# Three fused blocks on one core: q and k fetched ahead of two moves, the last weight conversions split, token stores declared independent, and each expert's rows gathered a unit sooner

## The chip, the cores and the metric

The kernel runs on one core of a Trainium2 chip. A core has TensorE (PE in the rows; its weight loads are PEld), VectorE (DVE), ScalarE (ACT), GpSimd (POOL) and SyncE (SP), each with its own instruction queue, and 16 DMA engines that carry transfers between HBM and the on-chip memories. SP issues nearly all loads, POOL the transfers with indices and the stores of converted weights. The metric is device time in microseconds of one execution. Three runs of the kernel before gave 932.81 (median), 929.98 and 934.12.

## The reference

Attention with a causal mask and a bias from cumulative sums; its output, with heads side by side, is the token matrix of an expert layer (each token goes to the one expert with the largest logit), and that output goes through a dense feed-forward with a squared ReLU. The weights of the last block, `w_in` and `w_out`, arrive in float64; the rest is float32. q, k and v are (4, 8, 576, 64), s is (4, 8, 576), the tokens (2304, 512), the eight experts' `w1` (512, 1024) and `w2` (1024, 512) each, `w_in` (512, 2048), `w_out` (2048, 512).

```python
scores = scale * np.matmul(q, k.transpose(0, 1, 3, 2))
cum = np.cumsum(np.maximum(s, 0.0), axis=-1)
bias = -(cum[:, :, :, None] - cum[:, :, None, :])
scores = np.where(causal, -1e9, scores + np.minimum(bias, 0.0))
attn = softmax(scores);  out = np.matmul(attn, v)
e_idx = np.argmax(x @ w_gate, axis=1)
for e in range(E):
    ye = np.maximum(x[mask] @ w1[e], 0.0) @ w2[e]
    out[mask] = gate_w[mask, None] * eom[mask, e, None] * ye
r = np.maximum(x @ w_in, 0.0);  return (r * r) @ w_out
```

## The kernel before

Every float32 matmul operand is split into a high and a low part (`xt[:, 0]`, `xt[:, 1]`; `h`, `w` likewise), and three products are summed. The program has three stages, which follow each other.

**Attention (to about 250 us).** Work goes by 16 pairs of heads. For a pair, `load_qk` (lines 353 and 356) fetches q and k in four DMAs (for each, 128 x 2 x 256 and 64 x 2 x 64 floats), `order_qk` (line 373, on POOL in most pairs) lays them out as `qr` and `kr`, TensorE transposes them (lines 404, 408), and ScalarE and VectorE write the high and low parts into the two operand tiles `sta` and `stb`. The low and high rows are then spread within and between these tiles by DMAs on SP (`move`, line 441): three into `stb` from `sta` (`spread_b`), two within `sta` (`spread_a`). `load_aug` (lines 393, 394) adds the four rows of the bias to each tile. The score matmuls (line 490) read `sta` and `stb`; then come the maximum, the exponential, transposes of the probabilities (line 550) and the products with v (line 588). `load_v` is lines 380 and 383, the finished rows go to `x_d` in HBM at lines 726 and 730, and the first expert weights are brought in at line 253 (`stg`).

**Experts (255 to 505 us).** Eight experts, each with eight units of 128 hidden columns. `gather` (line 282, on POOL) brings the rows of an expert into `xr` by an index list, TensorE transposes them (line 1122), `emit_h` does the first product (line 1196), lines 1207 and 1208 take the ReLU and split `h`, `emit_y` does the second (line 1234). `put_tokens` (line 1390, on POOL) writes, by an index list, 20 blocks of the sorted list of tokens, `tok_d`, which the last stage needs. In the same stage VectorE, ScalarE and POOL turn the float64 weights into float32, in 32 pieces of 128 x 512: `cv_load` (SP), `cv_a` (line 1165 on VectorE, lines 1167 and 1168 on ScalarE: `cva`, `cvs`, `cvm`), `cv_b` (lines 1173, 1175 and 1177 on VectorE, then the products of lines 1178 and 1179 on POOL), `cv_store` (line 1184, a DMA on POOL into `w_in_d` or `w_out_d`). The expert weights come to `stg` (line 225) and are split into `w` (line 234 on ScalarE, line 238 on VectorE). The first 24 pieces are converted here, the last 8 in the next stage, where `cva`, `cvs` and `cvm` have one buffer each.

**Feed-forward (505 to 912 us).** Six tiles of 384 tokens, 16 units each: line 1196, then lines 1213 (ACT, `r`), 1214 (DVE, `r`), 1216 (ACT, `h`) and 1217 (DVE, `h`), then line 1241. Rows go to their tokens' places at line 1273, with a memset of a small tile `gap` between stores (line 1276).

**What sets the order.** Within a stage, each piece of work is put on a list with a number by `at(key, fn)`, and `emit_tasks` sorts the list and emits it; the instructions of each engine stand in that order. In the attention the numbers come from a table `K_` and the pair's base `t0`; a change of `ldqk` moves `load_qk` of every pair whose number is not bounded by the ordering of the pair two before. In the other stages a number is a count of units. A tile framework adds the semaphore waits: an instruction waits for those whose data or buffers it needs, and a DMA that writes a tensor waits for an earlier DMA that writes the same tensor.

Of the kernel before, what the change touches and what calls it, by code (L numbers as in the profile page):

```python
# [18 lines left out]
AF = mybir.ActivationFunctionType  # L19
# [26 lines left out]
    order=[0, 1, 3, 11, 2, 10, 4],  # L46
# [2 lines left out]
    LE=1.22,  # L49
    LV=0.63,  # L50
    vact=[[0], [1], [1], [1], [0], [1], [1, 1]],
    ldqk=-13.2,
    ldv=-3.41,
    scq=-4.19,
    sck=-5.35,
# [16 lines left out]
    cvb=0.4,  # L72
# [14 lines left out]
def attention_moe_ffn_kernel(  # L87
# [122 lines left out]
    def at(key, fn, *args):  # L210
        tasks.append((key, len(tasks), fn, args))
# [84 lines left out]
    with tc.manual_schedule():  # L296
# [862 lines left out]
        def cv_a(n):  # L1159
            t = cv[n][0]  # L1160
            a = cv_p.tile([P, 512], I32, tag="cva", name="cva")
            sq = cv_p.tile([P, 512], F32, tag="cvs", name="cvs", bufs=2 if n < NCV else 1)
            m = cv_p.tile([P, 512], F32, tag="cvm", name="cvm", bufs=2 if n < NCV else 1)
            mid = t.rearrange("p n z -> p (n z)").bitcast(U16).rearrange("p (n z) -> p n z", z=4)[:, :, 1]
            nc.vector.tensor_scalar(
                out=a, in0=t[:, :, 1], scalar1=3, scalar2=0x3FFFFFFF, op0=ALU.logical_shift_left, op1=ALU.bitwise_and)
            nc.scalar.activation(out=sq, in_=t.bitcast(F32)[:, :, 1], func=AF.Square)
            nc.scalar.activation(out=m, in_=mid, func=AF.Copy, scale=2.0 ** -36)
            cv[n] += [a, sq, m]

        def cv_b(n):
            t, a, sq, m = cv[n]
            nc.vector.scalar_tensor_tensor(
                out=a, in0=t[:, :, 1], scalar=-0x40000000, in1=a, op0=ALU.bitwise_and, op1=ALU.bitwise_or)
            nc.vector.scalar_tensor_tensor(
                out=sq, in0=sq, scalar=2.0 ** -30, in1=a.bitcast(F32), op0=ALU.is_ge, op1=ALU.mult)
            nc.vector.tensor_single_scalar(out=a, in_=sq.bitcast(I32), scalar=-0x800000, op=ALU.bitwise_and)  # L1177
            nc.gpsimd.tensor_tensor(out=m, in0=m, in1=a.bitcast(F32), op=ALU.mult)  # L1178
            nc.gpsimd.tensor_tensor(out=m, in0=sq, in1=m, op=ALU.add)  # L1179
            cv[n] = m  # L1180
# [196 lines left out]
        def pos_tokens():  # L1377
# [7 lines left out]
                out=pos_i.rearrange("p b t -> p (b t)"), in0=x, in1=rk_all.rearrange("p b t -> p (b t)"), op=ALU.add)  # L1385
            nc.vector.tensor_copy(out=tok[:, :, :, 1].bitcast(F32), in_=gsq)

        def put_tokens(b, t):
            n = P if t < NB - 1 else TAIL
            nc.gpsimd.indirect_dma_start(  # L1390
                out=tok_d[:, :], out_offset=bass.IndirectOffsetOnAxis(ap=pos_i[0:n, b, t:t + 1], axis=0),
                in_=tok[0:n, b, t, :], in_offset=None)

        def get_tokens():
            nc.sync.dma_start(out=tok_m, in_=tok_d.rearrange("(m p) z -> p m z", p=P))
# [32 lines left out]
        for g in range(E):  # L1428
# [4 lines left out]
                for c in range(len(rows_of(g + 1))):  # L1433
                    x_trans(g + 1, c, n0 + K_['xt0'] + K_['xt1'] * c, 0.3)
            if g + 2 < E:
                at(n0 + 6.5, gather, g + 2)
            hj = half_jobs(g + 1, "a") + half_jobs(g + 1, "b")
            at(n0 + 2.15, alloc_next)
            at(n0 + 2.15, alloc_next)
# [11 lines left out]
        if wide:  # L1451
            for n in range(NCV):
                t = K_['cvp'] * n + K_['cv0']
                at(max(t - K_['cvl'], 0.0), cv_load, n)
                at(t, cv_a, n)
                at(t + K_['cvb'], cv_b, n)
                at(t + K_['cvb'] + 0.01, cv_store, n)
        at(NS - 11.4, load_xf, 0)
        at(NS - 7.7, xf_hi, 0)
# [30 lines left out]
        if wide:  # L1490
            for i, n in enumerate(range(NCV, len(pieces))):
                t = 2.1 * i + 1.5
                at(t - 1.6, cv_load, n)
                at(t, cv_a, n)
                at(t + 0.2, cv_b, n)
                at(t + 0.21, cv_store, n)
        for i, job in enumerate(half_jobs(E + 1, "a") + half_jobs(E + 1, "b")):
            ta = 3.5 + 2.1 * i if i < 4 else 6.9 + 4.2 * (i - 4)
            w_job(job, ta - 1.2, ta, ta + 0.3)
# [107 lines left out]
```

## Time and profile before

| | |
|---|---|
| median of three runs | 932.81 us (929.98 to 934.12) |
| profiled execution | 931.6 us, of it the span 929.7 us |
| TensorE busy | 867.6 us (93%) |
| VectorE, ScalarE, POOL busy | 528.6, 446.3, 283.8 us |
| mean granted clock of TensorE | 0.975 |
| moved by DMA | 123.87 MB, mean 133 GB/s |

Times are counted from the start of the span. In the rows, `q<-in_q_dram` reads "into q from in_q_dram", xN is the number of instructions that a row sums up, and what stands in brackets is the idle time of the engine just before and who ended it. A row of the windows gives the stretch and its length, then for PE, PEld, DVE, ACT and POOL the busy time and the instructions, then the granted clock, the busy share of the 16 DMA engines, and GB/s. The granted clock is a share of TensorE's full clock; 0.50 is the lower of its two levels.

### The profile page before, as it was taken

How to read it: one execution, taken by the hardware profiler on the slowest of the kernel's cores; microseconds unless marked ns; L12 is line 12 of the kernel's file. 1: busy time of each engine (PE TensorE's matmuls, PEld its weight loads, DVE VectorE, ACT ScalarE, POOL GpSimd, SP SyncE). 2: the span in 40 equal slices, each digit the busy share in tenths (PEclk: the TensorE clock that was granted, in tenths of full speed). 3: DMA queues.
4: the chain of work that ended last, by engine and by line, in shares of the span. 5: the costliest groups of instructions: out<-in, count | busy, mean ns of one | idle time of the engine just before them, and what ended most of it. 6: DMA issues, size and time to landing. Idle time of an engine off the chain costs nothing.

```text
span 929.7 us, 15091 instructions
## 1 busy us (share of the span) xinstructions
PE 867.6 (93%) x5397; PEld 761.8 (82%) x5397; DVE 528.6 (57%) x1166; ACT 446.3 (48%) x985; POOL 283.8 (31%) x311
## 2 busy tenths in 40 slices
PE   7999998889989999998987899999999999999992
PEld 5777766667589989998987798999999999989991
DVE  8777666667758787887695666332323322322220
ACT  6677677778436556555654444232322323222220
POOL 5333143532236577767540244011001001001001
PEclk9999899999999999999998999999999999999996
DMA  5667677777158888888966642220000100000001
GB/s 151 160 155 177 164 172 193 188 191 187 37 181 277 253 251 282 279 232 271 305 221 195 199 151 71 68 68 15 25 29 35 35 1 35 1 1 35 1 1 37
DMA packets 87572, 123.87 MB, mean 133 GB/s; under 512 B 33601, under 2 KB 58177, under 8 KB 86594
## 3 DMA queue, kind: packets, MB, share of 16 engines
q1 hardware_dynamic: 80978, 103.77, 40.4%
q0 software_dynamic: 6224, 18.01, 5.4%
q10 hardware_dynamic: 288, 1.05, 0.4%
q8 instruction: 45, 0.74, 0.3%
q14 instruction: 37, 0.30, 0.1%
HBM read 83.12 MB, written 23.17 MB: 114 GB/s over the span
## 4 chain that ended last, share of the span: by engine, by line
PE 32%; issue 30%; DMA 16%; ACT 6%; DVE 5%; POOL 4%; SPq 3%; POOLq 0%; DVEq 0%; ACTq 0%
PE z L1196 10%; PE z L1241 6%; DMA stb<-sta 4%; PE z L1234 3%; PE s L490 3%; DMA cv<-in_moe_w_in_dram 3%; PE t L588 3%; PE t L550 2%; DVE w L238 2%; ACT p L534 2%; POOL out_dram L1273 2%; DMA sta<-aug_d 1%; DMA cv<-in_moe_w_out_dram 1%; DMA stg<-in_moe_w_dram 1%; SPq L441 1%
## 5 line engine op out<-in xcount | busy, mean ns | idle before, releaser
L1196 PE MATMUL z<-xt,w 128*128 128x384 f32 (+6 forms) x1920 | 338.5, 325 | 6.3 <-DVE r L1214 3.0
L1196 PEld LDWEIGHTS z<-xt,w 128*128 128x128 f32 x1920 | 316.0, 190 | 16.3 <-DVE h L1208 3.4
L1241 PE MATMUL z<-w,h 128*128 128x512 f32 x864 | 214.9, 393 | 0.0
L1241 PEld LDWEIGHTS z<-w,h 128*128 128x128 f32 x864 | 160.7, 188 | 29.3
L1214 DVE SCALAR_TENSOR_TENSOR r<-z,r 128x384 f32<-128x384 f32 x96 | 53.3, 555 | 168.2 <-ACT r L1213 168.2
L1213 ACT ACTIVATE r<-z 128x384 f32<-128x384 f32 x96 | 47.0, 490 | 168.2 <-PE z L1196 166.4
L1234 PE MATMUL z<-h,w 128*128 128x304 f32 (+5 forms) x768 | 117.6, 302 | 8.2 <-ACT h L1207 5.9
L1234 PEld LDWEIGHTS z<-h,w 128*128 128x128 f32 x768 | 109.6, 191 | 9.4 <-ACT h L1207 6.3
L238 DVE TENSOR_TENSOR w<-stg,w 128x1024 fp32r<-128x1024 f32 x72 | 109.8, 1525 | 8.5 <-ACT w L234 8.2
L1273 POOL DMA_INDIRECT out_dram<-ysb,tok_m x18 | 17.4, 964 | 314.7 <-ACT ysb L1260 312.4
L234 ACT CAST w<-stg 128x1024 fp32r<-128x1024 f32 x72 | 75.5, 1049 | 70.5 <-DMA stg<-in_moe_w_dram 50.0
L1217 DVE TENSOR_TENSOR h<-r,h 128x384 fp32r<-128x384 f32 x96 | 56.7, 590 | 55.6 <-ACT h L1216 55.6
L534 ACT ACTIVATE p<-p,nm 128x128 f32<-128x128 f32 (+3 forms) x144 | 84.3, 590 | 4.2 <-DVE nm L517 4.1
L517 DVE CUSTOM_DVE_ANT_0 p<-s,mask 128x128 f32<-128x128 f32 (+3 forms) x128 | 59.8, 486 | 45.9 <-PE s L490 45.0
L1216 ACT CAST h<-r 128x384 fp32r<-128x384 f32 x96 | 49.3, 513 | 73.4 <-DVE r L1214 73.4
L1178 POOL TENSOR_TENSOR cvm<-cvm,cva 128x512 f32<-128x512 f32 x32 | 44.1, 1377 | 100.3 <-DVE cva L1177 59.1
L550 PE MATMUL t<-ident,p 128*128 128x128 f32 x400 | 69.5, 289 | 2.1 <-ACT pt L569 0.7
L490 PE MATMUL s<-sta 68*128 68x192 f32 (+7 forms) x204 | 51.7, 350 | 14.9 <-DMA sta<-aug_d 13.2
L550 PEld LDWEIGHTS t<-ident,p 128*128 128x128 f32 x400 | 47.1, 145 | 15.3 <-ACT p L534 7.2
L1179 POOL TENSOR_TENSOR cvm<-cvs,cvm 128x512 f32<-128x512 f32 x32 | 58.9, 1841 | 2.5
L588 PE MATMUL t<-pt,v 128*64 128x320 f32 (+4 forms) x448 | 53.1, 368 | 0.0
L569 ACT COPY pt<-t 128x512 f32<-128x512 f32 (+1 forms) x94 | 46.8, 514 | 12.2 <-PE t L550 7.1
(218 smaller groups left out, 957.3 us busy)
## 6 DMA issues: line engine op xcount, KB each, us to landing
stg<-in_moe_w_dram SPq DMA_DIRECT2D x56, 512.0 KB
cv<-in_moe_w_out_dram SPq DMA_DIRECT2D x16, 512.0 KB
stb<-sta SPq DMA_DIRECT2D x14, 576.0 KB
cv<-in_moe_w_in_dram SPq DMA_DIRECT2D x14, 512.0 KB
xr<-yT_d SPq DMA_DIRECT2D x6, 768.0 KB
q<-in_q_dram SPq DMA_DIRECT2D x16, 256.0 KB
k<-in_k_dram SPq DMA_DIRECT2D x16, 256.0 KB
v<-in_v_dram SPq DMA_DIRECT2D x32, 128.0 KB
```

The source lines that it names most:

```text
L234: nc.scalar.copy(out=w_parts(job)[0], in_=raw[job])
L238: nc.vector.tensor_tensor(out=lo, in0=raw.pop(job), in1=hi.bitcast(F32), op=ALU.subtract)
L490: nc.tensor.matmul(ps[0:mw, d0:d0 + nn], lhsT=ql[r, m0:m0 + mw], rhs=kl[r, c0:c0 + nn], start=(i == 0 and (tail or n == 0)), stop=(done an ...
L517: nc.vector.tensor_tensor_reduce(out=dst, in0=src, in1=msk, scale=-1.0, scalar=3.0e38, op0=ALU.add, op1=ALU.min, accum_out=nm[:, c:c + 1])
L534: nc.scalar.activation(out=pt[:, cs], in_=pt[:, cs], func=AF.Exp, scale=-1.0, bias=nm[:, c:c + 1], accum_out=rs[:, r:r + 1])
L550: nc.tensor.transpose(tp[:, i * P:(i + 1) * P], pt[:, j0:j0 + P], ident)
L588: nc.tensor.matmul(o[64 * hd:64 * hd + 64, c0:n], lhsT=vt[r0:P, jb, hd, :], rhs=pt[r0:P, hd, jb, c0:n], start=(jb == 0), stop=(jb == last))
L1179: nc.gpsimd.tensor_tensor(out=m, in0=sq, in1=m, op=ALU.add)
L1196: nc.tensor.matmul(ps[:, 0:n], lhsT=wa[:, zw, kk, fl * P:(fl + 1) * P], rhs=xt[:, zx, kk, 0:n], start=(i == 0), stop=(i == 3 * KD - 1))
L1217: nc.vector.tensor_tensor(out=ht[:, 1, 0:n], in0=gg, in1=ht[:, 0, 0:n].bitcast(F32), op=ALU.subtract)
L1234: nc.tensor.matmul(y_acc[g][d][:, 0:n], lhsT=wb[:, zw, fl, d * P:(d + 1) * P], rhs=ht[:, zh, 0:n], start=(f == 0 and i == 0), stop=(f == n ...
L1241: nc.tensor.matmul(acc, lhsT=ht[:, zh, c * P:(c + 1) * P], rhs=wb[:, zw, fl, :], start=(f == 0 and i == 0), stop=(f == nf - 1 and i == 2))
```

## The change

There are four edits.

1. `ldqk` goes from -13.2 to -16.83, so `load_qk` is emitted earlier than `spread_a` of the pair before.
2. `cv_a` and `cv_b` of a conversion are split: `cv_m` is ScalarE's scaling (`cvm`), `cv_c` POOL's two products. In the expert stage all stand where they stood. For the last eight pieces, `cv_m` goes from t to t + 1.15, the rest from t + 0.2 to t + 1.3 units.
3. Each store of tokens is declared independent of the stores before it (the positions are distinct), and a memset of `gap` follows each on POOL.
4. The gather for expert g + 2 goes from 6.5 to 5.5 units into expert g.

```diff
--- before.py
+++ after.py
@@ -49,7 +49,7 @@
     LE=1.22,
     LV=0.63,
     vact=[[0], [1], [1], [1], [0], [1], [1, 1]],
-    ldqk=-13.2,
+    ldqk=-16.83,
     ldv=-3.41,
     scq=-4.19,
     sck=-5.35,
@@ -1165,8 +1165,10 @@
             nc.vector.tensor_scalar(
                 out=a, in0=t[:, :, 1], scalar1=3, scalar2=0x3FFFFFFF, op0=ALU.logical_shift_left, op1=ALU.bitwise_and)
             nc.scalar.activation(out=sq, in_=t.bitcast(F32)[:, :, 1], func=AF.Square)
-            nc.scalar.activation(out=m, in_=mid, func=AF.Copy, scale=2.0 ** -36)
-            cv[n] += [a, sq, m]
+            cv[n] += [a, sq, m, mid]
+
+        def cv_m(n):
+            nc.scalar.activation(out=cv[n][3], in_=cv[n].pop(), func=AF.Copy, scale=2.0 ** -36)
 
         def cv_b(n):
             t, a, sq, m = cv[n]
@@ -1175,6 +1177,10 @@
             nc.vector.scalar_tensor_tensor(
                 out=sq, in0=sq, scalar=2.0 ** -30, in1=a.bitcast(F32), op0=ALU.is_ge, op1=ALU.mult)
             nc.vector.tensor_single_scalar(out=a, in_=sq.bitcast(I32), scalar=-0x800000, op=ALU.bitwise_and)
+            cv[n] = a, sq, m
+
+        def cv_c(n):
+            a, sq, m = cv[n]
             nc.gpsimd.tensor_tensor(out=m, in0=m, in1=a.bitcast(F32), op=ALU.mult)
             nc.gpsimd.tensor_tensor(out=m, in0=sq, in1=m, op=ALU.add)
             cv[n] = m
@@ -1385,11 +1391,17 @@
                 out=pos_i.rearrange("p b t -> p (b t)"), in0=x, in1=rk_all.rearrange("p b t -> p (b t)"), op=ALU.add)
             nc.vector.tensor_copy(out=tok[:, :, :, 1].bitcast(F32), in_=gsq)
 
+        tputs = []
+
         def put_tokens(b, t):
             n = P if t < NB - 1 else TAIL
-            nc.gpsimd.indirect_dma_start(
+            put = nc.gpsimd.indirect_dma_start(
                 out=tok_d[:, :], out_offset=bass.IndirectOffsetOnAxis(ap=pos_i[0:n, b, t:t + 1], axis=0),
                 in_=tok[0:n, b, t, :], in_offset=None)
+            nc.gpsimd.memset(gap, 0.0)
+            for old in tputs:
+                tc.declare_no_dep(put.ins, old.ins, reason="each token has its own place in the sorted order")
+            tputs.append(put)
 
         def get_tokens():
             nc.sync.dma_start(out=tok_m, in_=tok_d.rearrange("(m p) z -> p m z", p=P))
@@ -1433,7 +1445,7 @@
                 for c in range(len(rows_of(g + 1))):
                     x_trans(g + 1, c, n0 + K_['xt0'] + K_['xt1'] * c, 0.3)
             if g + 2 < E:
-                at(n0 + 6.5, gather, g + 2)
+                at(n0 + 5.5, gather, g + 2)
             hj = half_jobs(g + 1, "a") + half_jobs(g + 1, "b")
             at(n0 + 2.15, alloc_next)
             at(n0 + 2.15, alloc_next)
@@ -1453,7 +1465,9 @@
                 t = K_['cvp'] * n + K_['cv0']
                 at(max(t - K_['cvl'], 0.0), cv_load, n)
                 at(t, cv_a, n)
+                at(t, cv_m, n)
                 at(t + K_['cvb'], cv_b, n)
+                at(t + K_['cvb'], cv_c, n)
                 at(t + K_['cvb'] + 0.01, cv_store, n)
         at(NS - 11.4, load_xf, 0)
         at(NS - 7.7, xf_hi, 0)
@@ -1492,8 +1506,10 @@
                 t = 2.1 * i + 1.5
                 at(t - 1.6, cv_load, n)
                 at(t, cv_a, n)
-                at(t + 0.2, cv_b, n)
-                at(t + 0.21, cv_store, n)
+                at(t + 1.15, cv_m, n)
+                at(t + 1.3, cv_b, n)
+                at(t + 1.3, cv_c, n)
+                at(t + 1.31, cv_store, n)
         for i, job in enumerate(half_jobs(E + 1, "a") + half_jobs(E + 1, "b")):
             ta = 3.5 + 2.1 * i if i < 4 else 6.9 + 4.2 * (i - 4)
             w_job(job, ta - 1.2, ta, ta + 0.3)
```

TensorE's order is the same in both kernels. The first place is SP's queue in one of the later attention pairs; `sta_134` and `stb_136` are the pair's operand tiles, `in_q_dram` and `in_k_dram` the inputs. Before:

```order
L441 DMA stb_136<-sta_134 64x2304
L441 DMA stb_136<-sta_134 64x576 x2
L253 DMA stg<-in_moe_w_dram 128x512
L441 DMA sta_134<-sta_134 64x576 x2
L393 DMA sta_134<-aug_d 4x576
L394 DMA sta_134<-aug_d 4x576
L353 DMA q<-in_q_dram 128x2x256
L356 DMA q<-in_q_dram 64x2x64
L353 DMA k<-in_k_dram 128x2x256
L356 DMA k<-in_k_dram 64x2x64
L253 DMA stg<-in_moe_w_dram 128x512
```

and now:

```order
L441 DMA stb_136<-sta_134 64x2304
L441 DMA stb_136<-sta_134 64x576 x2
L353 DMA q<-in_q_dram 128x2x256
L356 DMA q<-in_q_dram 64x2x64
L353 DMA k<-in_k_dram 128x2x256
L356 DMA k<-in_k_dram 64x2x64
L253 DMA stg<-in_moe_w_dram 128x512
L441 DMA sta_134<-sta_134 64x576 x2
L393 DMA sta_134<-aug_d 4x576
L394 DMA sta_134<-aug_d 4x576
L253 DMA stg<-in_moe_w_dram 128x512
```

The four fetches stand ahead of the weight load and the two moves within `sta`, right behind the moves into `stb`. The same holds for ten pairs; in six of them no load of `stg` stands there.

The second place is POOL's queue in the expert stage, around the gather for expert 6 (`tok_d` is the token list, `xr` the gathered rows, `cvm` a conversion's result). Before:

```order
L1184 DMA w_out_d<-cvm 128x512
L1390 DMA tok_d<-tok,pos_i 2304x2 x2
L1178 TENSOR_TENSOR cvm<-cvm,cva 128x512
L1179 TENSOR_TENSOR cvm<-cvs,cvm 128x512
L1184 DMA w_out_d<-cvm 128x512
L1390 DMA tok_d<-tok,pos_i 2304x2
L1178 TENSOR_TENSOR cvm<-cvm,cva 128x512
L1179 TENSOR_TENSOR cvm<-cvs,cvm 128x512
L1184 DMA w_out_d<-cvm 128x512
L282 DMA xr<-x_d,tbl_p 128x512 x2
L282 DMA xr<-x_d,tbl_p 16x512
```

and now:

```order
L1190 DMA w_out_d<-cvm 128x512
L1398 DMA tok_d<-tok,pos_i 2304x2
L1401 MEMSET gap 128x1
L1398 DMA tok_d<-tok,pos_i 2304x2
L1401 MEMSET gap 128x1
L1184 TENSOR_TENSOR cvm<-cvm,cva 128x512
L1185 TENSOR_TENSOR cvm<-cvs,cvm 128x512
L1190 DMA w_out_d<-cvm 128x512
L282 DMA xr<-x_d,tbl_p 128x512 x2
L282 DMA xr<-x_d,tbl_p 16x512
L1398 DMA tok_d<-tok,pos_i 2304x2
L1401 MEMSET gap 128x1
```

The three DMAs of the gather stand ahead of a token store and of a conversion's products and store, where they stood behind them. The gathers for experts 3 and 7 move past a token store and a conversion in the same way; those for experts 4 and 5 keep their place among the conversions.

The third place is ScalarE's queue in the feed-forward, around the second of the last eight conversions (numbers tell buffers apart; `cv` is the piece as loaded). Before:

```order
L234 CAST w2_6680<-stg_6864 128x1024
L1167 ACTIVATE cvs_6896<-cv_6862 128x512
L1168 ACTIVATE cvm_6897<-cv_6862 128x512
L1213 ACTIVATE r_6905<-z6_6872 128x384
L1216 CAST h_6904<-r_6905 128x384
L1213 ACTIVATE r_6943<-z7_6916 128x384
L1216 CAST h_6942<-r_6943 128x384
L234 CAST w3_6681<-stg_6901 128x1024
L234 CAST w2_6680<-stg_6940 128x1024
L1167 ACTIVATE cvs_6974<-cv_6938 128x512
L1168 ACTIVATE cvm_6975<-cv_6938 128x512
```

and now:

```order
L234 CAST w2_6700<-stg_6877 128x1024
L1167 ACTIVATE cvs_6916<-cv_6875 128x512
L1219 ACTIVATE r_6924<-z6_6892 128x384
L1222 CAST h_6923<-r_6924 128x384
L1171 ACTIVATE cvm_6917<-cv_6875 128x512
L1219 ACTIVATE r_6957<-z7_6929 128x384
L1222 CAST h_6956<-r_6957 128x384
L234 CAST w3_6701<-stg_6920 128x1024
L234 CAST w2_6700<-stg_6953 128x1024
L1167 ACTIVATE cvs_6994<-cv_6951 128x512
L1219 ACTIVATE r_6999<-z6_6963 128x384
```

The scaling into `cvm` stands behind the next tile's `r` and `h`, where it stood right behind the square into `cvs`.

## Rows read from the trace of the kernel before

**Rows 1.** Waits on TensorE: waited for, total us, times, longest.
```profile
PE s L490 <- DMA sta<-aug_d: 13.2, 7, 2.8
...
PE z L1122 <- DMA xr<-x_d,tbl_p: 5.4, 3, 4.1
PE z L1196 <- DVE r L1214: 3.0, 1, 3.0
```

**Rows 2.** SyncE's timeline, three stretches: start, us, line, DMA, pieces.
```profile
59.02 3.61 SPq L441 DMA_DIRECT2D stb<-sta  x3
...
116.73 3.62 SPq L441 DMA_DIRECT2D stb<-sta  x3
122.66 1.11 SPq L441 DMA_DIRECT2D sta<-sta  x2
...
124.72 0.40 SPq L353 DMA_DIRECT2D q<-in_q_dram  x1
...
127.21 0.59 SPq L253 DMA_DIRECT2D stg<-in_moe_w_dram  x1
...
136.37 0.83 SPq L253 DMA_DIRECT2D stg<-in_moe_w_dram  x1
138.35 1.10 SPq L441 DMA_DIRECT2D sta<-sta  x2
...
194.69 3.54 SPq L441 DMA_DIRECT2D stb<-sta  x3
```

**Rows 3.** Windows: busy us (count) by engine, granted clock, DMA share, GB/s.
```profile
59.00:194.70 135.70, 121.90 (x914) 90.90 (x912) 89.15 (x323) 96.38 (x280) 46.41 (x57) 0.95 0.75 178
194.70:218.70 24.00, 23.95 (x192) 17.56 (x191) 18.15 (x62) 19.85 (x56) 9.01 (x8) 1.00 0.81 194
122.50:123.50 1.00, 1.00 (x11) 0.83 (x9) 0.93 (x8) 0.74 (x3) 0.12 (x1) 1.00 0.03 8
126.50:127.00 0.50, 0.50 (x4) 0.42 (x5) 0.00 (x0) 0.00 (x0) 0.00 (x0) 1.00 0.85 275
...
422.50:425.90 3.40, 3.22 (x14) 3.23 (x15) 1.03 (x3) 2.03 (x4) 1.89 (x2) 0.51 1.05 340
```

**Rows 4.** POOL's timeline, 313 to 334 us; idle before in brackets.
```profile
321.55 0.98 POOL L1390 DMA_INDIRECT tok_d<-tok,pos_i  x1 [6.01 <-DVE h L1208]
...
326.68 1.03 POOL L282 DMA_INDIRECT xr<-x_d,tbl_p  x1 [0.31 <-issue]
...
331.12 1.66 POOL L1390 DMA_INDIRECT tok_d<-tok,pos_i  x1 [0.31 <-issue]
```

**Rows 5.** The list of waits on POOL: the token stores.
```profile
POOL tok_d L1390 <- DMA tok_d<-tok,pos_i: 15.6, 6, 4.6
```

**Rows 6.** Groups by line on POOL: busy us, mean ns, idle before.
```profile
L1179 POOL TENSOR_TENSOR cvm<-cvs,cvm 128x512 f32<-128x512 f32 x32 | 58.9, 1841 | 2.5
L1178 POOL TENSOR_TENSOR cvm<-cvm,cva 128x512 f32<-128x512 f32 x32 | 44.1, 1377 | 100.3 <-DVE cva L1177 59.1 <-ACT h L1207 11.5 <-issue 11.0
...
L1276 POOL MEMSET gap<- 128x1 f32 x18 | 2.1, 115 | 0.0
```

**Rows 7.** The chain of waits, two stretches: start, us, what.
```profile
314.03 6.77 DMA tok_d<-tok,pos_i
...
415.18 7.45 DMA xr<-x_d,tbl_p
```

**Rows 8.** Timelines of VectorE and TensorE, 334 to 339 us.
```profile
334.13 0.43 DVE L1165 TENSOR_SCALAR cva<-cv 128x512 int32<-128x512 int32 x1 [2.23 <-POOL cvm L1178]
...
338.56 1.93 PE L1196 MATMUL z<-xt,w 128*128 128x304 f32 x12 [2.11 <-DVE h L1208]
```

**Rows 9.** Timelines of ScalarE and TensorE, 523 to 529 us.
```profile
523.35 0.66 ACT L1168 ACTIVATE cvm<-cv 128x512 f32<-128x512 uint16 x1 [2.80 <-DMA w_out_d<-cvm]
523.91 0.48 ACT L1213 ACTIVATE r<-z 128x384 f32<-128x384 f32 x1
...
525.03 3.86 PE L1196 MATMUL z<-xt,w 128*128 128x384 f32 x12 [3.00 <-DVE r L1214]
```

## The prediction

> **What bounds the kernel now.** I read the list of waits on TensorE first, because TensorE is the engine that sets the end, and asked of every long wait where it lies and who is late. The largest is 13.2 us in seven waits of the attention's score matmuls (line 490) for the loads of `sta`; the expert stage has 5.4 us in three waits of the row transposes (line 1122) for gathered rows; the start of the second feed-forward has one wait of 3.0 us for VectorE's `r` [rows 1]. The edits touch these three places and no other long wait, so I take them one by one.
>
> *Attention.* SyncE's timeline shows who paces a head pair. Behind the three moves that spread `stb` (issue ends at 116.73 + 3.62 = 120.35) SP stands still until they have landed and issues `sta` at 122.66: 2.31 us in which the queue does nothing. Only after `sta` come the four fetches of q and k, from 124.72 to 127.21, 2.49 us of issuing [rows 2]. In four late pairs a load of `stg` already stands in the wait (136.37, ends 137.20, `sta` at 138.35), which leaves 1.15 us of it [rows 2]. From the `stb` moves at 59.02 to those at 194.69 there are nine pairs in 135.67 us, 15.1 us each [rows 2]; the last two pairs, which have no q and k left to fetch, take 24.00 us, 12.0 each [rows 3]. TensorE is busy 121.9 of the nine pairs' 135.7 us at a granted clock of 0.95 and 23.95 of the last 24.00 us at 1.00 [rows 3]. So with the fetch in the queue SP sets the pair and TensorE waits; without it TensorE is the bound.
>
> *Experts.* POOL is one queue for token stores (line 1390), gathers (line 282) and the two conversion products (lines 1178, 1179). A store waits for the store ahead of it to land: issued at 314.03, landed 6.77 us later [rows 7], the next starts at 321.55 [rows 4]. The page names another releaser there, which had long been done, so I go by the landing. Six such waits come to 15.6 us [rows 5]. Two of them reach TensorE: a VectorE conversion waits 2.23 us for POOL at 334.13 and TensorE 2.11 us at 338.56 behind it [rows 8]; and the gather for expert 6 goes out only at 415.18, lands 7.45 us later [rows 7], and is the 4.1 us of [rows 1]. After that wait TensorE is granted 0.51 for 3.4 us [rows 3], the lower level (1.2 GHz).
>
> *Start of the second feed-forward.* `cvm` has one buffer; ScalarE's write of it at 523.35 waits 2.80 us for the store of the piece before, and the `r` that TensorE needs stands right behind it at 523.91; TensorE starts at 525.03 after 3.00 us, and slowly (3.86 us for 12 matmuls) [rows 9]. From 545 us on the feed-forward waits for nothing that an edit moves.
>
> **A: q and k fetched in front of `sta`.** Nothing is added or taken away: ten times four DMAs on SP, 2.49 us of issue, go into the wait for `stb`. In six pairs the free 2.31 us take nearly all of it, `sta` slips by about 0.2, and SP's loop is 2.2 us shorter; in the four late pairs 1.15 us are free, the loop is 1.2 shorter and `sta` is issued about 1.3 later. If SP alone set the pair: 6 × 2.2 + 4 × 1.2 = 18.0 us. The other end is lower than this. The q and k data now lie ahead of `sta` on the way to SBUF: two pieces of 128 x 2 x 256 and two of 64 x 2 x 64 floats are 0.59 MB, 2.1 us at the 275 GB/s at which they land now and 3.3 us at the stretch's mean of 178; the DMA engines are nearly idle in the wait (share 0.03 at 122.5 to 123.5), so about 1 us of that is free [rows 3]. So `sta` lands about 1 us later in an early pair and nearly 2 in a late one, a delay that eats the lead of the pairs but is paid again in each pair only where `sta`'s landing is itself the loop (the first rival). What TensorE can give back is the 13.2 us of waits and some of the lower clock behind them. I take 1.5 of 2.2 us in the early pairs and 0.6 of 1.2 in the late ones, where the DMA share is already 0.75 [rows 3]: 6 × 1.5 + 4 × 0.6 = 11.4, less part of the one slip: **−11 us**, range −5 to −15.
>
> **B: token stores that don't wait, gathers a unit sooner.** The 20 stores lose the wait for the one before; a memset of 0.115 us follows each, 2.3 us in all on POOL [rows 6], which idles elsewhere. The second store goes at about 315.6 instead of 321.55. But the gather of expert 3 (from 326.68 to 331.12, 4.4 us [rows 4]) now stands ahead of the store and the products that were at 321.55, so these start only 1 to 1.5 us sooner; the next products come some 5 us sooner, and the 2.23 us of VectorE and the 2.11 us of TensorE go: −2.1. The gather of expert 6 stands one store and one pair of products (1.4 + 1.8 us [rows 6], and a store) sooner, and the waits of the stores ahead of it are gone: out of 415.18 by at least 6 us, so that its 7.45 us of landing end before TensorE asks. That takes the 4.1 us, and half of the 3.4 us at half clock: −1.7. Together **−8 us**. Bounds: −4, where the gather's landing lengthens since more transfers run together (the landing of one gather is all I see), and −10, where the other waits for gathers (5.4 − 4.1 = 1.3 us) and a little clock come too.
>
> The landing is the row on which this rests: 6.77 us [rows 7]. The Trainium skill (DMA: Bandwidth & Descriptors, section Anatomy of one DMA — SWDGE (gpsimd) path) puts the fixed cost of a GpSimd DMA at about 2.0 us whatever its size; by that a store of a kilobyte would be down before the next starts, declaring the stores independent would be worth nothing, and the sum would be 2.1 us higher. This trace has three times that, so the row decides.
>
> **C: the last eight conversions later and in pieces.** ScalarE's scaling of the middle bits (`cvm`) moves from right behind the square to behind the next tile's `r` and `h`, and the bit work and products with it. The 3.0 us at 525.03 go with the clock drop behind them (1.7, by the 3.4 us at half clock of [rows 3]): −4.7. What is new: `cvs` and `cva` have one buffer as well, and the products of a piece, now later, must be done on POOL (3.2 us by the means [rows 6]) before ScalarE may square the next piece; the next `r` is queued behind that square, and TensorE waits for `r`. The store that is late at the start (it lands at about 523.3) pushes one piece into the next, so I expect two waits of nearly the POOL pair, 2.9 us each, until the pieces have caught up: +5.8. Bounds: −4.7 (no new wait) and +7 (two whole pairs, 6.4 us, and a clock drop behind each, 3.4, less 4.7 is 5.1; one store that lands late again adds about 2). Together **+1 us**, between ends far apart, since the wait that goes and those that come are of one kind and size.
>
> **Sum.** The profiled execution took 931.6 us (span 929.7 and 1.9 around it). 931.6 − 11 − 8 + 1 = 913.6; that execution lies 1.2 us under the median of 932.8, so 914.8, rounded to **915 us**. I add the terms whole, for the three stages follow each other and none overlaps another.
>
> **Rivals.** (1) *Slower: the fetch lengthens the pair.* `sta` can be issued only when `stb` is down and must land before the score matmuls; with 0.59 MB ahead of it this path grows by 2.1 − 1.0 = 1.1 us in ten pairs and by another 0.95 us in the four where 0.26 MB of `stg` is ahead too (at 275 GB/s): 11 + 3.8 = +14.8 in place of −11. With B and C: 932.8 + 14.8 − 7 = 941 us. It decides where the landing of `sta`, not SP's queue, closes the loop of a pair. For it speaks that TensorE's waits end on `sta` [rows 1]; against it that the last two pairs have the same moves and take 12 us [rows 3], and that the engines idle in the wait. The Trainium skill (DMA: Bandwidth & Descriptors, section Queues, rings and completion order) says that on each DMA engine the descriptors of one issuer are consumed in ring order, which is the premise of this rival: `sta` can't overtake the fetch. The share of 0.03 in [rows 3] shows the ring empty at that time, so the trace bears out only part of it. (2) *Attention gains nothing*: ScalarE's and VectorE's chains or the transfers take the place of SP. ScalarE is busy 96.4 of 135.7 us, the DMA engines 0.75 of it [rows 3], so there is room, but little in the late pairs. 932.8 − 7 = 926 us. (3) *The last conversions wait more often*: C is +5: 919 us. (4) *The stores wait all the same* (a bound on DMAs in flight, or the next gather behind them): then only the gathers' −5.8 are left of B: 917 us.
>
> **Chances.** Forecast 0.52, (1) 0.09, (2) 0.18, (3) 0.13, (4) 0.08. The forecast's own range is 906 to 922, from half of A's and C's bounds. For 8 in 10 the range reaches down to 903 (A −15, B −10, C −4.7 make 902 to 903) and up to 930, past (2) with a little of its spread; most of (1) stays out. A measurement of this kernel tells about 0.5% (4.7 us) from no change. Faster by more: nearly all of the forecast, (3) and (4) and four fifths of (2): 0.82. Within: the rest of (2) and a weak form of (1): 0.10. Slower: 0.08.
>
> **What would show it.** A: SP's timeline has q and k between `stb` and `sta`, the pairs are about 13.5 us apart, and the waits of line 490 for `sta` fall well below 13 us; if they grow, rival (1) is right. B: stores on POOL follow each other without a wait of 4 to 6 us, the gather of expert 6 goes out before 410 us on this trace's clock, and no granted clock of 0.5 stands near 422. C: no wait of TensorE for `r` at the first conversion but two shorter ones within the next 25 us. The forecast is wrong if the attention ends less than 5 us sooner, or if the feed-forward takes over 6 us more from its first matmul to its last.

## The result and the profile after

The changed kernel takes 919.9 us (median of four runs, 918.3 to 920.7) against 933.5 of the kernel before in the same comparison: a ratio of 0.986 with a 95% interval of 0.983 to 0.990, so 13.6 us or 1.4% faster. The forecast was 915, from 903 to 930. The profiled execution took 918.3 us, its span is 916.4.

TensorE's instructions stand in the same order in both kernels, so each matmul of one trace can be set beside the same matmul of the other. The difference of their starts, by place:

| the same matmul, before | after | ahead by | what lies between |
|---|---|---|---|
| 205.4 us | 192.9 | 12.5 | attention |
| 313.0 | 300.6 | 12.4 | experts 0 and 1 |
| 343.3 | 329.0 | 14.3 | the wait of [rows 8] |
| 424.3 | 404.2 | 20.1 | the gather for expert 6 |
| 464.7 | 451.5 | 13.2 | experts 6 and 7 |
| 513.3 | 497.8 | 15.5 | end of the experts |
| 529.9 | 509.7 | 20.2 | the first of the last conversions |
| 599.9 | 586.6 | 13.3 | the other conversions; constant from here on |

The gains came where the sum had put them, and two of them were partly given back within 50 us. Waits on TensorE, columns as in [rows 1]:

```profile
PE z L1240 <- ACT h L1213: 8.6, 3, 5.2
PE s L490 <- DMA sta<-aug_d: 5.9, 5, 2.8
PE z L1202 <- DVE r L1220: 4.0, 3, 2.3
...
PE z L1122 <- DMA xr<-x_d,tbl_p: 1.2, 1, 1.2
```

The waits for `sta` fell from 13.2 to 5.9 us and those for gathered rows from 5.4 to 1.2. The waits for `r` (3.0 before) grew, and so did those for ScalarE's `h`, which [rows 1] doesn't carry. Before they were:

```profile
PE z L1234 <- ACT h L1207: 5.9, 2, 5.1
```

The longest of them, 5.1 us at 495 us, is there in both kernels. (Lines behind the edits moved: 1196, 1207, 1208, 1214, 1234 and 1390 are now 1202, 1213, 1214, 1220, 1240 and 1398.)

**Attention.** SyncE's timeline of a pair, where [rows 2] had a standstill:

```profile
109.29 3.63 SPq L441 DMA_DIRECT2D stb<-sta  x3
113.02 0.74 SPq L353 DMA_DIRECT2D q<-in_q_dram  x1
...
115.24 0.65 SPq L356 DMA_DIRECT2D k<-in_k_dram  x1
116.33 1.15 SPq L441 DMA_DIRECT2D sta<-sta  x2
...
122.67 3.63 SPq L441 DMA_DIRECT2D stb<-sta  x3
```

From 112.92 to 116.33 SP issues the four fetches; only 0.44 us are left of the wait. The pair is 13.4 us long. The nine pairs that took 135.7 us in [rows 3] take 124.2 now, with TensorE at the full clock:

```profile
56.40:80.00 23.60, 23.48 (x182) 16.85 (x180) 15.81 (x55) 18.64 (x56) 7.85 (x8) 1.00 0.77 182
56.40:180.60 124.20, 116.96 (x925) 87.06 (x923) 91.01 (x326) 96.50 (x283) 48.40 (x58) 1.00 0.82 194
180.60:206.10 25.50, 25.39 (x200) 18.43 (x199) 19.41 (x66) 21.41 (x63) 9.00 (x8) 1.00 0.80 186
```

Of the 11.5 us, 6.6 are idle time that went (13.8 to 7.2 us beside the busy time), and 4.9 are busy time: 117.0 us instead of 121.9, for rather more matmuls (925 against 914), at a granted clock of 1.00 instead of 0.95. By `sta` and `stb` moves, five early pairs take 66.3 us (56.42 to 122.67) instead of 73.7 (59.02 to 132.75), 1.5 less each, and the four late ones 57.9 instead of 61.9, 1.0 less each.

**Experts.** On POOL the stores follow each other, and the gather for expert 6 goes out at 391.44:

```profile
380.57 1.01 POOL L1398 DMA_INDIRECT tok_d<-tok,pos_i  x1 [0.30 <-issue]
381.58 0.26 POOL L1401 MEMSET gap<- 128x1 f32 x1
381.88 0.97 POOL L1398 DMA_INDIRECT tok_d<-tok,pos_i  x1
...
391.44 1.11 POOL L282 DMA_INDIRECT xr<-x_d,tbl_p  x1 [0.30 <-issue]
```

That is 23.7 us sooner than the 415.18 of [rows 7], 11 more than the attention gave. TensorE takes these rows at 403.37 without a wait, and then stops for something else:

```profile
403.37 0.60 PE L1122 MATMUL z<-ident,xr 128*128 128x128 f32 x4
...
431.32 2.23 PE L1240 MATMUL z<-h,w 128*128 128x288 f32 x12 [2.91 <-ACT h L1213]
...
442.74 1.77 PE L1202 MATMUL z<-xt,w 128*128 128x272 f32 x12 [0.91 <-DVE h L1214]
```

The chain of waits of the changed kernel says what `h` was late for (start, us, what):

```profile
407.49 9.05 DMA stg<-in_moe_w_dram
...
418.32 1.23 DVE w L238
...
419.65 0.38 SPq L225
...
420.08 9.60 DMA cv<-in_moe_w_in_dram
...
430.34 0.64 ACT cvm L1171
430.98 0.30 ACT h L1213
```

A load of weights takes 9.05 us to land. SP's next load of weights (line 225) goes out only behind VectorE's conversion of it, the load of a conversion piece is queued on SP behind that, and it takes 9.60 us. ScalarE squares that piece and scales it ahead of `h`, and TensorE waits 2.91 us. The DMA engines are full in this stretch, and behind the wait the clock is granted at half (windows, columns as in [rows 3]):

```profile
433.10:436.50 3.40, 3.40 (x17) 3.40 (x16) 3.33 (x5) 3.15 (x7) 1.60 (x2) 0.50 0.53 166
410.00:420.00 10.00, 9.47 (x72) 9.06 (x71) 6.67 (x11) 4.52 (x10) 7.09 (x7) 1.00 1.00 271
420.00:430.00 10.00, 7.92 (x59) 7.42 (x57) 6.69 (x9) 3.06 (x6) 5.54 (x6) 1.00 0.90 252
```

**Last conversions.** ScalarE's timeline, which answers to [rows 9]:

```profile
506.95 0.68 ACT L1171 ACTIVATE cvm<-cv 128x512 f32<-128x512 uint16 x1 [0.68 <-DMA w_out_d<-cvm]
...
514.67 0.68 ACT L1167 ACTIVATE cvs<-cv 128x512 f32<-128x512 f32 x1 [4.57 <-POOL cvm L1185]
515.25 0.47 ACT L1219 ACTIVATE r<-z 128x384 f32<-128x384 f32 x1
```

The wait of 2.80 us for the store is 0.68 us now, but the next square waits 4.57 us for POOL's products, with `r` right behind it. TensorE waits for that `r`, and once more at 527.30:

```profile
516.37 2.37 PE L1202 MATMUL z<-xt,w 128*128 128x384 f32 x12 [1.44 <-DVE r L1220]
...
527.30 3.07 PE L1202 MATMUL z<-xt,w 128*128 128x384 f32 x12 [2.29 <-DVE r L1220]
```

### The profile page after: what moved, and what is told of

It is laid out like the page before. It is cut to its first block, busy times and chain, and to the rows that moved or that the text cites. A ratio compares the mean times of both kernels' runs of the same rounds, so it can differ in the third digit from the quotient of the medians.

```text
span 916.4 us, 15088 instructions
## 1 busy us (share of the span) xinstructions
PE 862.0 (94%) x5397; PEld 755.3 (82%) x5397; DVE 533.0 (58%) x1166; ACT 444.2 (48%) x985; POOL 284.0 (31%) x331
## 3 DMA queue, kind: packets, MB, share of 16 engines
q10 hardware_dynamic: 288, 1.05, 0.3%
## 4 chain that ended last, share of the span: by engine, by line
issue 33%; PE 26%; DMA 11%; DVE 10%; POOL 8%; ACT 5%; SPq 3%; POOLq 0%; DVEq 0%; ACTq 0%
PE z L1202 7%; DVE w L238 4%; PE z L1247 4%; PE z L1240 3%; DMA stg<-in_moe_w_dram 3%; PE s L490 3%; PE t L588 3%; PE t L550 2%; DMA sta<-aug_d 2%; POOL out_dram L1279 2%; POOL cvm L1185 1%; POOL cvm L1184 1%; DVE cva L1175 1%; SPq L441 1%; DVE cvs L1177 1%
## 5 line engine op out<-in xcount | busy, mean ns | idle before, releaser
L238 DVE TENSOR_TENSOR w<-stg,w 128x1024 fp32r<-128x1024 f32 x72 | 113.7, 1579 | 14.4 <-ACT w L234 14.4
L1240 PEld LDWEIGHTS z<-h,w 128*128 128x128 f32 x768 | 109.7, 191 | 11.5 <-ACT h L1213 9.3
L1223 DVE TENSOR_TENSOR h<-r,h 128x384 fp32r<-128x384 f32 x96 | 54.7, 569 | 55.6 <-ACT h L1222 52.7
L1184 POOL TENSOR_TENSOR cvm<-cvm,cva 128x512 f32<-128x512 f32 x32 | 42.1, 1316 | 123.4 <-DVE cva L1179 78.7
L550 PE MATMUL t<-ident,p 128*128 128x128 f32 x400 | 67.4, 281 | 2.2 <-ACT pt L569 0.7
L1185 POOL TENSOR_TENSOR cvm<-cvs,cvm 128x512 f32<-128x512 f32 x32 | 61.3, 1917 | 2.5
L550 PEld LDWEIGHTS t<-ident,p 128*128 128x128 f32 x400 | 45.2, 141 | 15.8 <-ACT p L534 7.9
```

What stands on the lines that cost most here:

```text
L238: nc.vector.tensor_tensor(out=lo, in0=raw.pop(job), in1=hi.bitcast(F32), op=ALU.subtract)
L550: nc.tensor.transpose(tp[:, i * P:(i + 1) * P], pt[:, j0:j0 + P], ident)
L1223: nc.vector.tensor_tensor(out=ht[:, 1, 0:n], in0=gg, in1=ht[:, 0, 0:n].bitcast(F32), op=ALU.subtract)
L1240: nc.tensor.matmul(y_acc[g][d][:, 0:n], lhsT=wb[:, zw, fl, d * P:(d + 1) * P], rhs=ht[:, zh, 0:n], start=(f == 0 and i == 0), stop=(f == n ...
```

## The experiments

Each ratio is to the kernel before in the same comparison; 0.1% is 0.93 us. Where a part stands alone, the rest is as before (in the runs of the four edits' parts the conversion helper is split but emitted where it was).

**q and k alone.**

```diff
-    ldqk=-13.2,
+    ldqk=-16.83,
```

> Of the four edits only the first (q and k fetched in front of the moves within sta); the conversion helper is split as in the changed kernel but emitted where it was. Theory (SP's queue sets the pair, and the fetch now hides in its wait): the attention ends 12 to 13 us sooner as in the changed kernel, the expert stage and the feed-forward are as long as before, so 12 to 13 us under the kernel before, about 921 us where the kernel before has 933.5. Rival (the expert stage is paced by transfers that run on their own clock, so that an earlier start is partly lost there): only 8 to 10 us. If the gain of the whole change came from the other edits: under 5 us.

Measured: 920.8 us, ratio 0.986 (0.982 to 0.991), some 13 us faster. That is the theory's figure, but the interval, 9 to 17 us, holds the upper half of the rival's 8 to 10 too. In the trace the attention is 11.6 us ahead at 205 us; the waits for gathers and `h`, still there, take part of it in the experts (5.3 ahead at 408, 7.5 at their end), and 9.2 are left at the end of the kernel, as the rival has it. So the attention's gain is shown, and whether the experts let all of it through is not.

**v in the wait instead of q and k.**

```diff
-    ldv=-3.41,
+    ldv=-2.85,
```

> The kernel before with one number changed: the three v fetches of a pair (0.29 MB, 2.6 us of issuing on SP) move from ahead of the stb moves into the wait between the stb and the sta moves, so v is fetched a little later than before; q and k stay where they were, behind sta. Theory (what counts is SP's issue time that leaves its loop, whatever is fetched): about 10 to 13 us under the kernel before, and SP's waits for stb at line 441 fall from 20.9 us to a few. Rival (what counts is that q and k arrive earlier): no gain, within 2 us of the kernel before. Second rival (0.29 MB ahead of sta delays its landing and that closes the loop): slower than before.

Measured: 921.5 us, ratio 0.987 (0.983 to 0.991), as much as with q and k, though v is fetched later and q and k stay where they were. SP's timeline:

```profile
109.10 3.67 SPq L441 DMA_DIRECT2D stb<-sta  x3
112.81 1.71 SPq L380 DMA_DIRECT2D v<-in_v_dram  x2
114.56 0.65 SPq L383 DMA_DIRECT2D v<-in_v_dram  x1
115.32 1.18 SPq L441 DMA_DIRECT2D sta<-sta  x2
```

The wait for `stb` no longer stands among SP's waits of the attention, and the nine pairs take 124.1 us, as with q and k alone (124.0), against 135.7 before. So it is SP's issue time that counts, not which data come sooner. This is the run that tells the two apart. (The profiled execution took 929.6 us, 8 over the median: it is 11.2 us ahead at 205 us, the experts take most of it back, and 2.2 are left.)

**Both in the wait.** Both numbers changed.

> The kernel before with both numbers of the attention changed: v, q and k of a pair (0.88 MB, some 5 us of issuing) all stand between the moves into stb and those within sta, where SP's queue waits only 2.3 us. Theory (SP's issue time sets the pair, and in the changed kernel SP no longer waits for stb, so nothing is left to hide): as q and k alone, 12 to 14 us under the kernel before. Rival (the fetch ahead of sta lengthens the path of a pair, and with q and k alone it was just short of deciding): sta is issued about 2.6 us later and lands 2 to 3 us later, the waits of TensorE for sta at line 490 grow to over 13 us, and the kernel is at least 8 us slower than with q and k alone.

Measured: 927.6 us, ratio 0.994 (0.990 to 0.997): faster than before, and 7 us (0.74%) slower than with q and k alone; the waits for `sta` are 10.0 us, against 5.8 with q and k alone. The early pairs are as short as with q and k alone (13.5 us here). The four late pairs, with the load of `stg` in the queue too, take 63.1 us (122.34 to 185.47), against 57.6 with q and k alone (122.38 to 180.01) and 61.9 before. My theory's "nothing is left to hide, so nothing changes" is wrong there. A late pair with q and k alone, on SP and TensorE:

```profile
137.27 3.58 SPq L441 DMA_DIRECT2D stb<-sta  x3
...
144.63 1.14 SPq L441 DMA_DIRECT2D sta<-sta  x2
...
149.98 0.45 PE L490 MATMUL s<-sta 68*128 68x192 f32 x2 [1.45 <-DMA sta<-aug_d]
```

and here:

```profile
138.15 3.63 SPq L441 DMA_DIRECT2D stb<-sta  x3
...
148.32 1.15 SPq L441 DMA_DIRECT2D sta<-sta  x2
...
153.95 0.45 PE L490 MATMUL s<-sta 68*128 68x192 f32 x2 [1.41 <-DMA sta<-aug_d]
```

From the moves into `stb` to those within `sta` it is 10.2 us instead of 7.4, and from there to the matmul that waits for `sta` 5.6 instead of 5.4. In the four late pairs `sta` goes out 2.3 to 3.7 us later, and where TensorE waits for it in both runs its landing takes 0.1 to 0.9 us more. So it is SP's issue time again, some 5 us in a wait of 2, that makes `sta` late, as the rival has it, and only to a small part the bytes ahead of it. The waits stayed under the rival's 13 us; its "at least 8 us" can't be told from the 7. What the bytes do shows with q and k alone: in the late pairs `sta` lands 5.4 to 5.5 us behind its issue, where it took 3.7 to 3.9 before with no fetch ahead. The Trainium skill (DMA: Bandwidth & Descriptors, section Queues, rings and completion order) has descriptors of one issuer consumed in ring order on each DMA engine. The late pairs are in line with that. The same section lets a later one finish its write before an earlier one, so the "can't overtake" of rival (1) is more than it states.

**Stores and gathers alone.** The third and fourth edit of the diff.

> Of the four edits only the third and fourth (token stores independent, gathers a unit sooner). Theory (the gathers' wait goes, and later waits for loads of weights and of conversion pieces, which share the DMA engines, take most of it back): the row transposes' waits of 5.4 us go to about 1, TensorE is 7 to 8 us ahead just behind the gather of expert 6, and 2 to 4 us are left at the end of the expert stage: 930 us where the kernel before has 933.5. Rival (the giving back in the changed kernel comes from its attention being shorter, not from these edits): 7 to 8 us are left, 926 us.

Measured: 928.6 us, ratio 0.995 (0.993 to 0.998), about 4.4 us faster by the ratio: the theory's 3.5 lies inside the interval, the rival's 7.5 does not. The trace shows the giving back without the shorter attention: 1.2 us ahead at 408 (in the kernel before's time), 6.9 at 424, 2.3 at 465, 4.7 at the end.

**Stores alone.** The third edit.

> Of the four edits only the third (token stores declared independent, with a memset behind each; gathers where they were). Theory (most of the gathers' lateness comes from stores that wait in front of them on POOL): 4 to 6 us under the kernel before, nearly as much as stores and gathers together (5.7), TensorE's wait for the gather of expert 6 gone or under 1.5 us. Rival (the place of the gathers does it): within 1.5 us of the kernel before, the wait of 4 us for the gather stays.

Measured: 925.3 us, ratio 0.992 (0.989 to 0.995), 5 to 10 us: the stores are most of the two, as the theory has it, and the gain is rather more than it asked for. The profiled execution took 931.8 us (the runs go from 921.4 to 931.8) and shows no gain at the end, so where the gain lies can't be read from it; in it the wait for gathered rows is 2.6 us at most instead of 4.1, so it shrank and did not go.

**Gathers alone.** The fourth edit.

> Of the four edits only the fourth (gathers from 6.5 to 5.5 units). Theory (the stores are most of it, as stores alone gave 6.8 us): 0 to 3 us under the kernel before; the gather of expert 6 stands past one store and one conversion, so its wait of 4.1 us on TensorE falls to under 1, and part of it is caught by later waits. Rival (either of the two is enough, the gain is the same wait): 5 to 7 us.

Measured: 930.4 us, ratio 0.998 (0.994 to 1.001): inside the 0 to 3 us of the theory, not clear of zero. In the trace the waits for gathered rows are not among the long ones, and TensorE gets 4.4 us ahead at the gather of expert 6 (between 408 and 424), all of them given back by 464 us. Stores alone are no worse than stores and gathers together; the overlap of the intervals leaves open whether the fourth edit adds anything.

**Last conversions alone.** The second edit.

> Of the four edits only the second (the last eight conversions later and in pieces). Theory (one wait of 3 us goes with its low clock, new waits for cvs buffers and the products come, more in sum): 1 to 3 us slower than the kernel before, with two or three waits of TensorE for r of 1 to 2.5 us each in the first 30 us of the feed-forward. Rival (the edit is a gain and the feed-forward's loss in the changed kernel comes from the stores still in flight behind a shorter expert stage): 1 to 4 us faster.

Measured: 934.5 us, ratio 1.002 (0.999 to 1.005): from 1.4 us faster to 4.4 slower. In the trace the wait of 3 us and its low clock go (4.8 us gained by the same matmuls from 513 to 530), two waits for `r` come, 3.2 us in sum, and 5.7 us are lost from there to 600: 0.9 us in sum, as C has it (−4.7 and +5.8).

**All but the conversions.** The second edit undone in the changed kernel.

> The changed kernel with the second edit undone (the last eight conversions back at their places; first, third and fourth edits stay). If the times add up as the parts did alone (about 13 us for the q and k fetches, 5 to 6 for stores and gathers): 18 to 19 us under the kernel before, about 915 us, 4 to 5 under the changed kernel. Theory that the expert stage gives back in company (behind the gathers TensorE runs into loads that are no sooner): 15 to 16 us under the kernel before, about 918 us, with a single wait for r at the start of the feed-forward as in the kernel before.

Measured: 915.4 us, ratio 0.982 (0.979 to 0.985), 16.9 us faster than before. With the changed kernel's 0.986 (0.983 to 0.990) the second edit cost about 4 us; the intervals just overlap. Parts apart (0.9861 and 0.9953) make 0.9815, so they may well add up; but the interval, 14 to 19.5 us, holds the 18 to 19 of adding up and the 15 to 16 of my theory alike.

**Bit work early.** In the changed kernel, for the last eight pieces:

```diff
-                at(t + 1.3, cv_b, n)
-                at(t + 1.3, cv_c, n)
-                at(t + 1.31, cv_store, n)
+                at(t + 0.2, cv_b, n)
+                at(t + 1.16, cv_c, n)
+                at(t + 1.17, cv_store, n)
```

> The changed kernel with VectorE's bit work (cv_b) of the last eight conversions back at t + 0.2, while the scaling stays at t + 1.15 and the products and the store come right behind it (t + 1.16, t + 1.17). Theory (the new waits come from products that are late for the single buffer of cvs, because the bit work stands late on VectorE): ScalarE's waits for POOL in front of the square (4.6 and 2.0 us in the changed kernel) go to about 1, TensorE's waits for r fall from 4.0 us to under 1.5, and the kernel is 3 to 5 us faster than the changed one, 915 to 917 us. Rival (the store that lands late sets it, whatever the products do): as the changed kernel, within 1 us.

Measured: 916.4 us, ratio 0.982 (0.978 to 0.985). The same rows of ScalarE, and POOL's first product (lines 1183, 1184 and 1218 are 1184, 1185 and 1219 of the changed kernel):

```profile
510.12 0.67 ACT L1171 ACTIVATE cvm<-cv 128x512 f32<-128x512 uint16 x1
510.88 1.28 POOL L1183 TENSOR_TENSOR cvm<-cvm,cva 128x512 f32<-128x512 f32 x1 [5.27 <-DVE h L1222]
...
513.57 0.68 ACT L1167 ACTIVATE cvs<-cv 128x512 f32<-128x512 f32 x1 [0.31 <-POOL cvm L1184]
514.15 0.47 ACT L1218 ACTIVATE r<-z 128x384 f32<-128x384 f32 x1
```

POOL's first product in the changed kernel:

```profile
511.74 1.28 POOL L1184 TENSOR_TENSOR cvm<-cvm,cva 128x512 f32<-128x512 f32 x1 [7.51 <-DVE cva L1179]
```

The square waits 0.31 us for POOL instead of 4.57, and TensorE's waits for `r` fall from 4.0 to 2.0 us (the theory asked for under 1.5). POOL starts the products 0.1 us behind the scaling (510.88), where in the changed kernel 4.1 us lay between (506.95 + 0.68 to 511.74) and POOL waited for the bit work (`cva`). By the same matmuls the stretch from 513 to 600 gains 1.4 us, where the changed kernel loses 2.2. So it was the late bit work that made the second edit a loss. With it mended the edit is no gain either: 916.4 us, against 915.4 with the edit undone.

**load_xf(1) later.** In the changed kernel:

```diff
-        at(NS - 7.0, load_xf, 1)
+        at(NS - 2.3, load_xf, 1)
```

> The changed kernel with the load of the second feed-forward tile's tokens (xr<-yT_d, load_xf(1)) moved on SP from ahead of the store of expert 6's rows (yT_d<-ysb) to behind the loads of the first feed-forward weights. Theory (what is won by the gathers is caught at the end of the expert stage, where the store waits 5 to 6 us for that load to land and the weight loads queue behind it, so that TensorE waits 5.2 us for h): that wait and its low clock go, 4 to 7 us under the changed kernel, 913 to 916 us. Rival (DMA supply sets the weights' landing there, the engines being full): the wait stays or moves, within 1.5 us of the changed kernel.

Measured: 916.2 us, ratio 0.983 (0.980 to 0.985), 3 to 4 us under the changed kernel. The chain of the changed kernel had, at this place:

```profile
467.23 5.77 DMA xr<-yT_d
...
473.11 0.40 SPq L1275
...
473.63 5.88 DMA stg<-w_in_d
```

a load, the store that waits for it, and the weights behind both; the wait for `h` was 5.2 us. With the load moved the waits for `h` (line 1213) fall from 8.6 to 2.4 us, and TensorE gains 6.6 us between 484 and 504 (0.9 in the changed kernel; this execution took 912.0 us, so its trace has more of the gain than the median). Of the 25.3 us that it is ahead there 5.6 are gone at 600. The first 2.2 are lost by 513, ahead of the last conversions' waits, and they are the moved load's own:

```profile
482.08 1.48 ACT L1144 CAST xt<-xr 128x1536 fp32r<-128x1536 f32 x1 [1.35 <-DMA xr<-yT_d]
483.46 0.48 ACT L1219 ACTIVATE r<-z 128x384 f32<-128x384 f32 x1
...
485.87 2.35 PE L1202 MATMUL z<-xt,w 128*128 128x384 f32 x12 [1.71 <-DVE r L1220]
```

The load now lands late for ScalarE, which splits its rows ahead of the next `r`, and TensorE waits 1.71 us. Behind it the last conversions do as in the changed kernel (6.8 us lost from 530 to 600, 7.0 there; ScalarE's squares wait 10.5 us for POOL, 10.0 there). But most of the gathers' gain was gone by 464 us, ahead of this place, in the traces of the changed kernel and of stores and gathers alone: the half of my theory that has it caught here is wrong; the wait was a loss of its own.

**Both mends**, and **conversions back with load_xf(1) later.**

> The changed kernel with both of the mends tried apart: the bit work of the last eight conversions at t + 0.2 with scaling, products and store behind it, and load_xf(1) behind the first feed-forward weights. Theory (the waits are in different places and add up): 915.7 x the gains of each apart, 3 to 4 us each, so 22 to 26 us under the kernel before, 907 to 911 us. Rival (with the expert stage ending sooner the stores of conversions land relatively later and the feed-forward takes it back): 16 to 18 us under the kernel before, as each alone.

> The changed kernel with the second edit undone and load_xf(1) behind the first feed-forward weights. Theory as in the run with the bit work early: 22 to 25 us under the kernel before; the one wait for r at the first conversions stays (about 3 us). Rival (that wait grows by what was won): 17 to 19 us under the kernel before.

Measured: 911.5 us, ratio 0.978 (0.974 to 0.983), for the first, the lowest median of all; 914.7 us, 0.982 (0.977 to 0.987), for the second. The theory asked for 22 to 26 us in the first; 20 came, and the interval (16 to 25) holds both sides. The first beats both given kernels; that it beats each mend alone isn't clear of the intervals. In the second the theory's 22 to 25 us did not come: it is 17 us faster (12 to 21), as the rival has it, and no better than with the conversions back alone (915.4 us). Its trace has the rival's reason: the wait for `r` at the first conversions is 4.2 us, where it is 1.9 with the conversions back alone, and the moved load brings a wait of 1.3 us as above.

## Why the prediction was right

**A, −11: right, and for the reason given.** −12.5 in the trace at 205 us, −13 alone by the medians. SP's issue time set the pair: the run with v in place of q and k gains the same. I had the pair at 13.5 us; it is 13.8 on the mean. By pairs, the early ones gave 1.5 us each as forecast, the late ones 1.0 where I had 0.6: that is where A was set too low. Part of the agreement is luck. The wait of 2.31 us that I took for all early pairs is the longest of the five from 59 to 132 us (1.8 to 2.3), and the fetches take 2.9 to 3.4 us to issue in the changed kernel, not 2.49, so `sta` goes out about 1.2 us later, not 0.2. The 1.5 was a choice out of 2.2; what limits an early pair now is TensorE, busy 23.48 us of the stretch from 56.40 to 80.00. And the clock, which I counted as "some", is 4.9 of the 11.5 us.

**Rival (1): half real, and not deciding.** Behind the fetch `sta` lands 5.3 to 6.3 us after its issue in the late pairs of the changed kernel, 3.7 to 3.9 before: 1.4 to 2.4 us more, where I had "nearly 2". In the one early pair that shows it (TensorE's wait at 119.78 with q and k alone) it is 3.75 us, no later than before, where I had 1. That fitted. With 0.88 MB ahead the late pairs lengthen by 5.5 us in sum, but mainly since `sta` is issued later, which is the queue of A and not the bytes of this rival. The margin of the late pairs was smaller than one v fetch more.

**B, −8: the place was right, the size not.** The two waits and the low clock behind them went, 1.9 + 5.5 = 7.4 us in the trace, against 2.1 + 4.1 + 1.7. The step that failed is "the waits go, so the time is won": 6.9 us were given back between 424 and 465, and 4.4 us alone (2 to 7) and 3 in the changed kernel's trace were left. Just behind the gather of expert 6 TensorE is ahead of its weights and of the conversion pieces on ScalarE's queue. New waits of 2.9, 1.2 and 0.9 us and another 3.4 us at half clock come within 40 us. I had priced a later gather as the danger, not the loads of the same stretch, whose DMA share of 0.86 to 1.05 in the trace of before was a warning. Whether it is the engines' supply or the place of the pieces in ScalarE's order was not tried: a stage with lighter loads would tell. How the 15.5 us at the end of the experts split between A and B is open as well: the trace of q and k alone loses 4.1 of its 11.6 us in the experts, and if the changed kernel's attention gain shrank there too, B is worth up to 7 in company; the medians with and without it (915.4 us, ratio 0.982, and 920.8, ratio 0.986, both without the second edit) make it 4, give or take 5.

**C, +1: both halves near, the sum on the low side.** The wait and its clock: −4.8 in the trace, −4.7 forecast. The new waits: +7.0 by the same matmuls, +5.8 forecast; of these the waits for `r` are 4.0, and nearly all the rest is matmuls that take longer (the granted clock is 0.93 from 509 to 535). Alone the edit came out at +0.9, close to the forecast; by the medians with and without it it cost 4 us in company, not clear of the trace's 2.2. The step had the right chain (late products, single buffer, square, `r`), and the run with the bit work early shows it.

**The sum.** −12.5 − 3.0 + 2.2 = −13.3 on the profiled executions, −18 forecast: A short by 1.5, B over by 5, C short by 1.2. That the total came within 5 us is partly luck, since A's error hides some of B's; and an error of 1 to 2 us in one pair of traces says little (below). Rival (2) is out, since the attention gained all; rival (3) half came true; rival (4) is out, since no store waits for another.

## What to carry to other kernels

In an in-order issue queue a wait is room: what is issued into it costs little, whatever it is, as long as the issuing nearly fits; what runs over sends the next transfer out later. Here 2.4 to 3.4 us in a wait of 2 shortened the pairs, and some 5 us, with a load of weights besides, made the late pairs longer than before. So fill the room, and measure where it is full. A wait that is taken away in a stage whose DMA engines are full may come back at the next load, as 6.9 us of lead did here: count what is won after the next 50 us, not at the place. When one step of a chain with single buffers is put off, put off only the step that was in the way, and compare with putting off none.

## What was unexpected

Programs with the same attention differ there from one execution to the next: at the matmul that starts at 122.1 us in the trace of before, the kernel with only its stores changed is 2.8 us behind, the one with only its gathers changed 2.0 us ahead. A term under 3 us can't be read from one pair of traces. A token store of 1 KB took 6.77 us to land [rows 7], and loads of 512 KB took 9 to 10 us where the DMA share was 0.9 to 1.0.
